# Drawn rows of V fetched by SyncE transfers with a register for the row, keys in natural order, steps in a new order

## The chip, the cores and the metric

One NeuronCore of a Trainium2 chip. The metric is the device time of one execution in microseconds (us): the median of three executions.

## The reference, cut to what matters

Block-sparse attention over 4 batches and 8 heads, and a feed-forward layer on its output. A block is 32 tokens, so a sequence of 768 has 24 blocks.

```python
scores = (1.0 / np.sqrt(D)) * np.matmul(q, k.transpose(0, 1, 3, 2))    # B, H, S, D = 4, 8, 768, 64
mask = np.abs(blk_i - blk_j) <= 1
mask = mask | (blk_i == 0) | (blk_j == 0) | (blk_i == n_blocks - 1) | (blk_j == n_blocks - 1)
for qb in range(n_blocks):
    for kb in sampled_blocks[qb]:                                      # three drawn blocks to a block
        mask[qb * block:(qb + 1) * block, kb * block:(kb + 1) * block] = True
...
attn_out = np.matmul(softmax(scores where mask), v)
x = attn_out.transpose(0, 2, 1, 3).reshape(B * S, H * D)               # 3072 x 512
h = x @ w_in                                                           # 512 x 2048
out = (h * np.cos(h)) @ w_out                                          # 2048 x 512
```

Which blocks are drawn is an input (`sampled_blocks`, 24 x 3), so their addresses are known only when the kernel runs.

## The kernel before

**Tiles.** The list `seq` has 24 tiles: in each of the 4 batches five sparse tiles of 128 query rows (four blocks, called groups below), and a dense one for the first and the last query block and what is left. Two tiles make a pair, and each pair goes through the feed-forward layer: up projection `ph` (line 1648), h*cos(h), down projection `po` (line 1745). Wide numbers are kept as two fp16 halves, a high and a low one, so most matmuls run on each half.

**A sparse tile.** The queries `U` meet 256 keys in each group: the two end blocks, a window of three blocks of its own, and three drawn blocks. `sparse_scores` (line 1367) writes the scores `sp` to PSUM, VectorE adds the mask `bias` (line 1394), ScalarE takes the exponential into `P` (line 1416), ScalarE and VectorE split it into the halves of `ring` (lines 1433 and 1437), a transposing transfer on SyncE brings `ring` to `PT` (line 1456), and TensorE multiplies PT by `V` (line 1467). The result is normalised and transposed to `xT` by another transfer on SyncE (line 1511), and `xT` feeds `ph`. The keys `W` come by transposing transfers (line 1183), once a batch.

**V.** Each batch's V is stored in DRAM as fp16 halves, in a scratch `scr[b]` with rows of 2 KB. A tile's 128 partitions of V are read from there, with the keys of a group in an order of even tokens and then odd ones:

- `v_ends` (lines 1308 to 1311): the two end blocks, in four SyncE transfers of 16 rows for four groups. A V buffer keeps them through its batch, so they are fetched only for the first two tiles of a batch: 32 transfers.
- `v_window` (lines 1313 to 1316): two SyncE transfers of 48 rows for four groups, 40 in all.
- `v_dense` (lines 1303 to 1306): two SyncE transfers for each dense tile, 8 in all.
- `v_gather` (lines 1318 to 1326): the drawn blocks, four GpSimd gathers of 96 rows to a sparse tile, 80 in all. Their row numbers come from the tile `gidx`, which VectorE makes at the start (`const_a`, line 1018 among it, and `const_gidx`).

There are two V buffers, and tile n takes buffer n % 2: a load for tile n must wait until tile n-2 has been multiplied by V. The keys of drawn blocks are copied on VectorE and ScalarE (line 1189), with their column taken from a register: the registers are loaded by TENSOR_LOAD (line 998), and an address step (FUSED_REGOPS) stands ahead of each copy.

**What sets the order.** A planner (`plan_kernel`, with the inner `gather_v` and `load_regs`) makes 3229 steps. The table `POS` gives each step, by its number, a place in one order over all engines; buffers are handed out in that order, and every engine's instructions are written in it. Each engine then works through its own in order, and an instruction whose data isn't there holds up all behind it on its engine. SyncE issues all transfers but the gathers.

Of the kernel before, what the change touches and what calls it, by code (L numbers as in the profile page):

```python
# [13 lines left out]
F32 = mybir.dt.float32  # L14
I32 = mybir.dt.int32
# [5 lines left out]
P = 128  # L21
# [14 lines left out]
XE = [4, 4, 4, 4, 4]  # L36
LPE = [0, 0, 0, 0, 0, 0, 0, 0, 0, 0, 0, 0, 0, 0, 0, 0]
# [1794 lines left out]
```

## Time and profile before

| | |
|---|---|
| three executions | 869.81, 871.02 and 859.93 us |
| the profiled execution | 861.11 us, of which the span (first to last instruction) is 859.2 us |
| granted TensorE clock, mean over the span | 0.910 of full speed |

An engine's busy share is over the span. The chain that ended last is followed back from the last instruction, at each step to what released it; its shares tell where the end was set. "issue" there is time in which an engine waited for nothing that the profile shows, SPq is SyncE's queue of instructions, and "DMA PT<-ring" is time in which the next piece of the chain waited for that transfer. All times of rows are from the one profiled execution. A row's share of the DMA queues is of the time of 16 DMA engines together.

### The profile page before, as it was taken

The page shows a single profiled execution, that of the slowest core. Times are in us where ns is not written, and L with a number is a line of the kernel's source. Part 1 is how long each engine was busy: PE and PEld are TensorE (multiplying, and loading weights), DVE is VectorE, ACT ScalarE, POOL GpSimd, SP SyncE. Part 2 cuts the span into 40 slices and gives each one's busy share as a digit, 9 for nine tenths or more (in the row PEclk, how much of TensorE's full clock was granted, in tenths as well). Part 3 has the DMA queues.
Part 4 walks back from the last instruction along what each step waited for, and adds up shares of the span by engine and source line. Part 5 has one row for each costly group of instructions (what it writes and reads, how often), then busy time and mean ns, then how long its engine had stood idle before and what let it go on. Part 6 is the DMA issues. An engine that isn't in the chain of part 4 may idle for free.

```text
span 859.2 us, 26549 instructions
## 1 busy us (share of the span) xinstructions
PE 711.9 (83%) x10953; PEld 488.2 (57%) x10953; DVE 549.6 (64%) x1619; ACT 597.5 (70%) x1214; POOL 97.8 (11%) x123
## 2 busy tenths in 40 slices
PE   3543579899878789898798988999987969999995
PEld 2433456575565447666465656667654647667662
DVE  4987989798748656785386756667735544644221
ACT  2686768789748778899397788688954746865220
POOL 4330122000200111000201110100110210000000
PEclk9755569899999899999899999999988989999998
DMA  7999998989999999999999999997979896742100
GB/s 270 276 278 227 185 223 180 210 170 201 239 178 168 193 176 219 210 192 168 189 169 196 178 209 185 204 168 128 197 112 161 114 159 111 140 99 50 37 13 29
DMA packets 239794, 146.34 MB, mean 170 GB/s; under 512 B 203952, under 2 KB 204080, under 8 KB 239664
## 3 DMA queue, kind: packets, MB, share of 16 engines
q1 hardware_dynamic: 234544, 128.83, 78.3%
q0 software_dynamic: 5120, 15.73, 8.3%
q8 instruction: 87, 1.43, 0.8%
q14 instruction: 43, 0.35, 0.2%
HBM read 77.67 MB, written 12.58 MB: 105 GB/s over the span
## 4 chain that ended last, share of the span: by engine, by line
PE 41%; DMA 20%; DVE 16%; ACT 10%; issue 8%; SPq 3%; another core or an unknown queue 1%; DVEq 0%; ACTq 0%
PE ph L1648 17%; PE po L1745 16%; DMA PT<-ring 7%; PE sp L1367 4%; ACT P L1416 3%; DMA U<-U 2%; DMA W<-kn 2%; DVE P L1394 2%; DVE ring L1437 2%; DMA xT<-n 2%; PE xp L1467 2%; DMA qs<-in_q_dram 2%; DVE w L1100 1%; ACT L1416 1%; DVE n L1100 1%
## 5 line engine op out<-in xcount | busy, mean ns | idle before, releaser
L1648 PE MATMUL ph<-xT,w 128*128 128x256 f16 x2304 | 281.5, 281 | 20.7 <-DMA xT<-n 7.4
L1745 PE MATMUL po<-w,g 128*128 128x512 f16 x1152 | 271.0, 386 | 0.8 <-issue 0.6
L1648 PEld LDWEIGHTS <-w 128*128 128x128 f16 x2304 | 229.9, 101 | 65.5 <-issue 21.4
L1745 PEld LDWEIGHTS <-g 128*128 128x128 f16 x1152 | 111.1, 99 | 125.9 <-issue 11.2
L1416 ACT ACTIVATE P<-P,sm 128x256 f32<-128x256 f32 (+1 forms) x224 | 139.3, 623 | 28.1 <-DVE sm L1411 16.2
L1321 POOL DMA_INDIRECT V<-scr,gidx x80 | 80.4, 1006 | 593.8 <-PE xp L1467 380.5
L1665 ACT ACTIVATE g<-ph,sm 128x512 f32<-128x512 f32 x96 | 72.8, 773 | 78.2 <-PE ph L1648 75.1
L1437 DVE TENSOR_TENSOR ring<-P,ring 128x512 f16<-128x512 f32 (+1 forms) x144 | 89.4, 628 | 58.9 <-ACT ring L1433 56.3
L1367 PE MATMUL sp<-W,U 128*32 128x192 f16 (+1 forms) x2560 | 68.7, 245 | 53.2 <-issue 29.2
L1671 DVE SCALAR_TENSOR_TENSOR hs<-ph,sm,g 128x512 f32<-128x512 f32 x80 | 59.1, 748 | 69.6 <-ACT g L1665 69.4
L1433 ACT CAST ring<-P 128x512 f16<-128x512 f32 (+1 forms) x144 | 80.2, 567 | 22.4 <-DMA PT<-ring 20.2
L1367 PEld LDWEIGHTS <-U 128*32 128x32 f16 x2560 | 50.0, 107 | 71.6 <-issue 68.1
L1394 DVE CUSTOM_DVE_ANT_1 P<-sp,bias 128x256 f32<-128x256 f32 x160 | 61.5, 419 | 44.4 <-PE sp L1367 30.0
L1736 DVE TENSOR_TENSOR g<-hs,g 128x1024 f16<-128x1024 f32 x48 | 58.6, 1220 | 18.8 <-ACT g L1733 18.5
L1733 ACT ACTIVATE g<-hs 128x1024 f16<-128x1024 f32 x48 | 50.3, 1050 | 21.4 <-DVE hs L1671 21.3
L1467 PE MATMUL xp<-V,PT 128*32 128x64 f16 x3840 | 45.3, 201 | 22.1 <-DMA PT<-ring 14.1
L1467 PEld LDWEIGHTS <-PT 128*32 128x32 f16 x3840 | 38.7, 98 | 34.3 <-DMA PT<-ring 15.4
L1416 ACT ACTIVATION_READ_ACCUMULATOR P<-P,sm 128x1 f32 x224 | 41.8, 187 | 0.0
L1394 DVE CUSTOM_DVE_ANT_1 P<-sp,dbias 128x384 f32<-128x384 f32 x64 | 35.1, 552 | 6.7 <-PE sp L1378 4.4
L1665 ACT ACT_TABLE_LOAD x29 | 37.2, 1283 | 0.5
L1097 ACT ACTIVATE kn<-stage,sm 128x256 f16<-128x256 f32 (+1 forms) x41 | 20.3, 526 | 23.1 <-DMA W<-kn 12.4
L1416 ACT ACT_TABLE_LOAD x28 | 35.9, 1283 | 0.5
(165 smaller groups left out, 683.1 us busy)
## 6 DMA issues: line engine op xcount, KB each, us to landing
V<-scr SPq DMA_DIRECT2D x40, 384.0 KB
stage<-in_k_dram SPq DMA_DIRECT2D x12, 512.0 KB
w<-in_moe_w_in_dram SPq DMA_DIRECT2D x12, 512.0 KB
w<-in_moe_w_out_dram SPq DMA_DIRECT2D x12, 512.0 KB
V<-scr SPq DMA_DIRECT2D x8, 768.0 KB
scr<-n SPq DMA_DIRECT2D x21, 256.0 KB
qs<-in_q_dram SPq DMA_DIRECT2D x20, 256.0 KB
U<-U SPq DMA_DIRECT2D x40, 128.0 KB
```

The lines of the kernel that those rows point to most:

```text
L1321: self.nc.gpsimd.indirect_dma_start(self.v_groups(V)[:96, j, 0, :], None, self.scr[b][:, :], bass.IndirectOffsetOnAxis(ap=self.gidx[:, c : ...
L1367: mm(o, U[:, z, h, rows], k, start=(a == 0 and z == 0 and part == 0), stop=(a == 1 and z == 1 and part == 1), tile_position=(0, BLK * j),)
L1394: self.nc.vector.tensor_tensor_reduce(out=self.head_cols(n, a, Pt).rearrange("p (n c) -> p n c", c=hf), in0=self.head_cols(n, a, sp).rearr ...
L1416: self.nc.scalar.activation(Pv, Pv, AF.Exp, scale=qc[:, 4:5], bias=nb[:, bcol : bcol + 1], accum_out=sums[:, 2 * j + a : 2 * j + a + 1],)
L1433: self.nc.scalar.copy(hi, p)
L1437: self.nc.vector.tensor_tensor(lo, p, hi, ALU.subtract)
L1467: mm(xp[32 * j : 32 * j + 32, h, :], PT[:, 4 * a + 2 * l + c, 32 * j : 32 * j + 32], V[:, j, c, h, d0:d1], start=(a == 0 and c == 0 and x ...
L1648: self.nc.tensor.matmul(ph[:, ff, :], self.W1[p][:, wl, cc, c * P : (c + 1) * P], xT[:, xl * NCC + cc, :], start=(j == 0), stop=(j == len( ...
L1665: self.nc.scalar.activation(self.half_cols(g, h), ph.rearrange("p f t -> p (f t)"), AF.Sin, scale=self.turns[b][:, p : p + 1], bias=self.h ...
L1671: self.nc.vector.scalar_tensor_tensor(self.half_cols(hs, h), ph.rearrange("p f t -> p (f t)"), c, self.half_cols(g, h), op0=ALU.mult, op1= ...
L1736: self.nc.vector.tensor_tensor(g[:, 1024:2048], hs, g[:, 0:1024], ALU.subtract)
L1745: self.nc.tensor.matmul(po, g[:, gl, ff, t * P : (t + 1) * P], self.W2[p][:, wl, ff, :], start=(first and ff == half * hf and j == 0), sto ...
```

## The change

- **Drawn rows.** In place of a gather of 96 rows, three SyncE transfers of 32 rows (64 KB) each, one to a drawn block: `v_drawn`, 12 to a sparse tile, 240 in all. Each takes its source row from a register, and in front of each SyncE has one address step ("ISA" in the order).
- **Registers.** SyncE loads them by TENSOR_LOAD: for each of the five sparse tiles of a batch nine that are kept for the whole kernel (`SPR = 9`), and three that are loaded anew for each of the 20 sparse tiles. 25 loads. `const_regs` makes the rows of the drawn blocks (`sv`) with one more instruction; `const_gidx` and ten instructions of `const_a` go.
- **Natural order of keys.** An end block comes by one transfer of 32 rows (two to a tile, 16 in all), and a window's transfer has consecutive rows. So that scores meet V in this order, `sparse_scores` writes the even and the odd keys of drawn blocks and windows to every second column of PSUM, and `bias` is laid out to suit.
- **Order.** `POS` is a new table, of 3397 steps, and the orders of all engines differ from those before.

```diff
+SPR = 9
 POS = [
...
 def gather_v(n, pos):
         if i < 2:
             for x in range(2):
-                for y in range(2):
-                    op("SP", 0, pos, lambda x=x, y=y: e.v_ends(n, V.t, x, y), r=[scr[b]], w=[(V, ("e", x, y))], dma=0.3, name=f"vg{n}_1")
+                op("SP", 0, pos, lambda x=x: e.v_ends(n, V.t, x), r=[scr[b]], w=[(V, ("e", x))], dma=0.8, name=f"vg{n}_1")
...
         for j in range(4):
-            op("POOL", 1.03, ipos + 0.8 + j * 0.5, lambda j=j: e.v_gather(n, V.t, j), r=[scr[b], gidx], w=[(V, ("d", j))], dma=1.5, name=f"vi{n}_{j}")
+            for s in range(3):
+                x = 3 * j + s
+                if x == SPR:
+                    load_regs(i, 4, [by["ksc0s"], *[o for o in pl.ops[-400:] if o.name.startswith(f"vi{n - 1 - (n % 6 == 0)}_3_")]], ipos + 0.8)
+                op("SP", 0, ipos + 0.8 + j * 0.5, lambda j=j, s=s: e.v_drawn(n, V.t, j, s), r=[scr[b], regs[i, 3 + (x >= SPR)]], w=[(V, ("d", j, s))], dma=0.35, hw=0.5, name=f"vi{n}_{j}_{s}")
...
+    for i in range(NS):
+        load_regs(i, 3)
     load_v(0, pr["V0"])
...
+        nc.vector.tensor_scalar(self.sv, self.sx, BLK, None, op0=ALU.mult)
...
 def v_rows(self, b, tok, n, j=0):
-        return bass.AP(src.tensor, src.offset, [[2 * self.HD, n], [j * self.HD, 4], [1, self.HD]])
+        return bass.AP(src.tensor, src.offset, [[self.HD, n], [j * self.HD, 4], [1, self.HD]])
...
-    def v_ends(self, n, V, e, y):
-        b, hf = self.seq[n][0], BLK // 2
-        p = (96, 0)[e] + hf * y
-        self.nc.sync.dma_start(self.v_groups(V)[p : p + hf, :, e], self.v_rows(b, (self.S - BLK) * e + y, hf))
+    def v_ends(self, n, V, e):
+        b, p = self.seq[n][0], (96, 0)[e]
+        self.nc.sync.dma_start(self.v_groups(V)[p : p + BLK, :, e], self.v_rows(b, (self.S - BLK) * e, BLK))
...
-    def v_gather(self, n, V, j):
+    def v_drawn(self, n, V, j, s):
         b, i = self.seq[n]
-        c = 4 * i + j
-        self.nc.gpsimd.indirect_dma_start(
-            self.v_groups(V)[:96, j, 0, :],
-            None,
-            self.scr[b][:, :],
-            bass.IndirectOffsetOnAxis(ap=self.gidx[:, c : c + 1], axis=0),
-        )
+        to = self.v_groups(V)[BLK * s : BLK * s + BLK, j, 0, :]
+        x = 3 * j + s
+        reg = self.regs[i, 3][x] if x < SPR else self.regs[i, 4][x - SPR]
+        self.nc.sync.dma_start(to, self.scr[b][bass.ds(reg, BLK), :])
...
 def sparse_scores(self, n, unit, U, sp):
-                            o = bass.AP(t.tensor, t.offset, [list(t.ap[0]), [48, 2], [160, 2], [1, 48]])
+                            o = bass.AP(t.tensor, t.offset, [list(t.ap[0]), [1, 2], [160, 2], [2, 48]])
```

What the order makes of it is shown at three places of SyncE's queue. The first is its start. `stage` and `hs` take inputs (keys and v), `w1` the weights, `sm` the registers' source. Before:

```order
1 L1237 DMA qs0_93<-in_q_dram 128x512
2 L961 DMA xT0_111<-in_sampled_blocks_dram 128x144
3 L1142 DMA stage0_78<-in_k_dram 128x1024
4 L1142 DMA stage1_79<-in_k_dram 128x1024
5 L1546 DMA w1_3_67<-in_moe_w_in_dram 128x1024
6 L1142 DMA stage2_80<-in_k_dram 128x1024
7 L1546 DMA w1_3_67<-in_moe_w_in_dram 128x1024
8 L1142 DMA hs0_82<-in_v_dram 128x1024
```

and after:

```order
1 L1225 DMA qs0_92<-in_q_dram 128x512
2 L972 DMA xT0_110<-in_sampled_blocks_dram 128x144
3 L1130 DMA stage0_77<-in_k_dram 128x1024
4 L1130 DMA stage1_78<-in_k_dram 128x1024
5 L1130 DMA stage2_79<-in_k_dram 128x1024
6 L1530 DMA w1_3_67<-in_moe_w_in_dram 128x1024
7 L1010 TENSOR_LOAD sm_76
8 L1130 DMA hs0_81<-in_v_dram 128x1024
```

A load of registers stands seventh, ahead of the load of v into hs0, and all three loads of keys stand ahead of the weights.

The second place is the change from batch 0 to batch 1, where the first key transposes (W<-kn) of the new batch are issued. Loads of V for tiles 6 and 7 go to V0 and V1. Before:

```order
134 L1142 DMA stage0_78<-in_v_dram 128x1024
135 L1311 DMA V1_110<-scr1_126 16x4x1024 x2
136 L1237 DMA qs0_93<-in_q_dram 128x512
137 L1511 DMA_TRANSPOSE xT1_112<-n160_90 128x8x128
138 L1183 DMA_TRANSPOSE W_63<-kn0_88 128x4x128 x2
139 L1183 DMA_TRANSPOSE W_63<-kn1_89 128x4x128 x2
140 L1316 DMA V0_109<-scr1_126 48x4x1024
```

and after:

```order
262 L1310 ISA
263 L1310 DMA V0_108<-scr1_125 32x1024
264 L1310 ISA
265 L1310 DMA V0_108<-scr1_125 32x1024
266 L1753 DMA out_0_dram<-kn0_87 128x512
267 L1225 DMA qs0_92<-in_q_dram 128x512
268 L1310 ISA
269 L1310 DMA V1_109<-scr1_125 32x1024
270 L1310 ISA
271 L1310 DMA V1_109<-scr1_125 32x1024
272 L1303 DMA V0_108<-scr1_125 48x4x1024
273 L1171 DMA_TRANSPOSE W_63<-kn1_88 128x4x128 x2
```

Before, end rows of V, queries and an xT transpose came ahead of the first key transposes, and the drawn rows were on GpSimd. Now four drawn pieces (32x1024) and a window (48x4x1024) stand there.

The third is inside a batch, at tile 8's transposes of the probabilities (PT<-ring). Before:

```order
181 L1456 DMA_TRANSPOSE PT1_106<-ring1_102 128x8x128
182 L1456 DMA_TRANSPOSE PT3_108<-ring3_104 128x8x128
183 L1511 DMA_TRANSPOSE xT0_111<-n161_91 128x8x128
184 L1316 DMA V1_110<-scr1_126 48x4x1024
185 L1277 DMA U0_94<-U0_94 64x1024
186 L1316 DMA V1_110<-scr1_126 48x4x1024
187 L1237 DMA qs0_93<-in_q_dram 128x512
188 L1226 DMA scr2_127<-n160_90 128x1024
```

and after:

```order
372 L1440 DMA_TRANSPOSE PT1_105<-ring1_101 128x8x128
373 L1010 TENSOR_LOAD sm_76
374 L1310 ISA
375 L1310 DMA V1_109<-scr1_125 32x1024
376 L1265 DMA U1_94<-U1_94 64x1024
377 L1495 DMA_TRANSPOSE xT0_110<-n160_89 128x8x128
378 L1310 ISA
379 L1310 DMA V1_109<-scr1_125 32x1024
380 L1263 DMA U1_94<-U1_94 64x1024
381 L1440 DMA_TRANSPOSE PT0_104<-ring0_100 128x8x128
```

Between two PT transposes there are now a load of registers and two drawn pieces of V, with an address step in front of each; the xT transpose stands behind one of them.

## Rows read from the trace of the kernel before

**Rows 1.** Page, part 1, busy time of each engine.

```profile
PE 711.9 (83%) x10953; PEld 488.2 (57%) x10953; DVE 549.6 (64%) x1619; ACT 597.5 (70%) x1214; POOL 97.8 (11%) x123
```

**Rows 2.** Page, part 4, the chain that ended last, by engine and by line.

```profile
PE 41%; DMA 20%; DVE 16%; ACT 10%; issue 8%; SPq 3%; another core or an unknown queue 1%; DVEq 0%; ACTq 0%
PE ph L1648 17%; PE po L1745 16%; DMA PT<-ring 7%; PE sp L1367 4%; ACT P L1416 3%; DMA U<-U 2%; DMA W<-kn 2%; DVE P L1394 2%; DVE ring L1437 2%; DMA xT<-n 2%; PE xp L1467 2%; DMA qs<-in_q_dram 2%; DVE w L1100 1%; ACT L1416 1%; DVE n L1100 1%
```

**Rows 3.** Waits of the engines for V: us in total, times, longest.

```profile
PE xp L1467 <- DMA V<-scr: 4.9, 2, 4.4
PEld L1467 <- DMA V<-scr: 4.5, 1, 4.5
```

**Rows 4.** Timeline of SyncE, first and last of its 478 transfers: start, us.

```profile
0.72 0.42 SPq L1237 DMA_DIRECT2D qs<-in_q_dram  x1
...
807.36 41.33 SPq L1769 DMA_DIRECT2D out_dram<-ot  x5
```

**Rows 5.** Tile V, loads: duration ns min/median/max, first and last start us.

```profile
L1316 SPq DMA_DIRECT2D V<-scr x40: 313/572/1444, 48.8 to 702.5; - x40
L1311 SPq DMA_DIRECT2D V<-scr x32: 303/532/1628, 46.9 to 649.5; - x32
L1306 SPq DMA_DIRECT2D V<-scr x8: 427/462/526, 177.6 to 731.8; - x8
```

**Rows 6.** Tile PT, its transposes on SyncE.

```profile
L1456 SPq DMA_TRANSPOSE PT<-ring x140: 960/1280/6934, 59.9 to 784.4; - x140
```

**Rows 7.** Page, part 5, groups: count | busy us, mean ns | idle before.

```profile
L1321 POOL DMA_INDIRECT V<-scr,gidx x80 | 80.4, 1006 | 593.8 <-PE xp L1467 380.5
...
L1367 PE MATMUL sp<-W,U 128*32 128x192 f16 (+1 forms) x2560 | 68.7, 245 | 53.2 <-issue 29.2
```

**Rows 8.** Lines 998 and 1189, register loads and address steps.

```profile
L998 DVEq TENSOR_LOAD <-sm x10: 961/968/2150, 7.2 to 299.5; - x10
L998 ACTq TENSOR_LOAD <-sm x5: 1753/1764/1948, 7.1 to 25.9; - x5
...
L1189 DVEq FUSED_REGOPS  x164: 57/57/65, 42.0 to 669.9; - x164
```

**Rows 9.** Waits of SyncE's own queue.

```profile
SPq L1456 <- DVE ring L1437: 53.3, 22, 8.1
...
SPq L1316 <- PE xp L1467: 8.0, 3, 3.8
```

**Rows 10.** The chain in order of time: start us, us, engine, line.

```profile
114.94 7.89 DMA xT<-n
...
236.79 10.96 DMA W<-kn
250.34 5.05 DMA W<-kn
...
318.49 3.10 DMA xT<-n
...
555.55 5.06 DMA xT<-n
...
680.84 11.18 DMA PT<-ring
...
740.22 5.06 DMA PT<-ring
```

**Rows 11.** Page, part 3, DMA queues: packets, MB, share of 16 engines.

```profile
q1 hardware_dynamic: 234544, 128.83, 78.3%
q0 software_dynamic: 5120, 15.73, 8.3%
```

**Rows 12.** Timeline of GpSimd: start, us, line, tiles [idle before <-releaser].

```profile
228.77 0.92 POOL L1321 DMA_INDIRECT V<-scr,gidx  x1 [78.69 <-PE sp L1128]
...
237.78 0.92 POOL L1321 DMA_INDIRECT V<-scr,gidx  x1 [0.30 <-issue]
```

**Rows 13.** Line 1018, one of VectorE's small instructions at the start.

```profile
L1018 DVE TENSOR_SCALAR xT<-xT x1: 153/153/153, 11.3 to 11.3; 128x1 f32<-128x1 f32 x1
```

More of the change, by code (lines that the diff above doesn't have):

```diff
@@ L369, in plan_kernel @@
     Vs = [Val(None, t) for t in e.vbufs]
-    bias, dbias, gidx = (Val() for _ in range(3))
+    bias, dbias = (Val() for _ in range(2))
     regs = {}
@@ L374, in plan_kernel, with load_regs @@
     op("DVE", 0.15, -400, lambda: e.const_regs(tmp.t), r=[(tmp, 0)], w=[sxv], name="sx")
-    def load_regs(i, which, after=()):
+    def load_regs(i, which, after=(), pos=0.0):
         regs[i, which] = Val()
         x = pr["XD"][i]
-        eng, cost, p = (("DVE", 0.05 + 0.236 * XE[i], pr["RG"][i]), ("ACT", 0.05 + 0.236 * (12 - XE[i]), pr["RA"][i]), ("DVE", 0.05 + 0.236 * (x - XE[i]), 200.0 + i))[which]
+        eng, cost, p = (("DVE", 0.05 + 0.236 * XE[i], pr["RG"][i]), ("ACT", 0.05 + 0.236 * (12 - XE[i]), pr["RA"][i]), ("DVE", 0.05 + 0.236 * (x - XE[i]), 200.0 + i), ("SP", 0.05 + 0.236 * SPR, -200.0 + i), ("SP", 0.05 + 0.236 * (12 - SPR), pos))[which]
         op(eng, cost, p, lambda: e.load_regs(i, which), r=[sxv], w=[regs[i, which]], name=f"regs{i}_{which}", after=after)
@@ L386, in plan_kernel @@
     op("DVE", 0.7, -298, lambda: e.const_a(tmp.t), r=[(tmp, "pid")], w=[(tmp, "a")], name="const_a")
-    op("DVE", 0.3, pr["CG"], lambda: e.const_gidx(tmp.t), r=[(tmp, "a"), (tmp, 0)], w=[gidx], name="const_gidx")
     op("DVE", 0.8, pr["CG"], lambda: e.const_samples(tmp.t), r=[(tmp, 0)], w=[(tmp, "smp")], name="const_samples")
@@ L858 @@
     KD, KX = 192, 576
-    SMALL = 296 + 72 + 24
+    SMALL = 296 + 144 + 24
     kv = wc = None
@@ L899, in __init__ @@
         self.junk = pool.tile([P, 512], BF16, name="junk")
-        self.gidx = pool.tile([96, 4 * self.NS], I32, name="gidx")
         self.bias = pool.tile([P, self.NS, 16], BF16, name="bias")
@@ L943, in __init__ @@
         self.bcol = {x: self.col(1) for x in "abcd"}
-        self.sx = self.col(3 * self.NB).bitcast(I32)[0:1]
+        self.sx, self.sv = (self.col(3 * self.NB).bitcast(I32)[0:1] for _ in range(2))
         self.k_src, self.wi, self.wo = k, w_in.bitcast(I32), w_out.bitcast(I32)
@@ L998, in load_regs @@
         self.regs[i, which] = self.nc.values_load_multi_w_load_instructions(
-            self.sx[0:1, x + (0, XE[i], XE[i])[which] : x + (XE[i], 12, d)[which]],
-            engines=[(ENG.DVE, ENG.Activation, ENG.DVE)[which]],
+            (self.sx, self.sv)[which > 2][0:1, x + (0, XE[i], XE[i], 0, SPR)[which] : x + (XE[i], 12, d, SPR, 12)[which]],
+            engines=[(ENG.DVE, ENG.Activation, ENG.DVE, ENG.SP, ENG.SP)[which]],
             min_val=0,
-            max_val=(self.S - BLK) // 2,
+            max_val=(self.S - BLK) // (1 if which > 2 else 2),
             skip_runtime_bounds_check_because="the indices were clamped to the blocks that there are",
@@ L1007, in const_a @@
         nc, NB = self.nc, self.NB
-        pid, low, third, jint = (self.tv(t, 320 + x, 1) for x in range(4))
-        self.lowf, thirdf, jf = (self.tv(t, 324 + x, 1, dt=F32) for x in range(3))
+        pid, jint, jf = self.tv(t, 320, 1), self.tv(t, 323, 1), self.tv(t, 326, 1, dt=F32)
         self.jf = jf
-        nc.vector.tensor_scalar(low, pid, 15, None, op0=ALU.bitwise_and)
-        nc.vector.tensor_scalar(third, pid, 4, None, op0=ALU.arith_shift_right)
         nc.vector.tensor_scalar(jint, pid, 5, None, op0=ALU.arith_shift_right)
-        nc.vector.tensor_copy(self.lowf, low)
-        nc.vector.tensor_copy(thirdf, third)
         nc.vector.tensor_copy(jf, jint)
-        odd = self.tv(t, 327, 1, dt=F32)
-        nc.vector.tensor_scalar(odd, thirdf, 3.0, None, op0=ALU.is_ge)
-        nc.vector.scalar_tensor_tensor(thirdf, odd, -3.0, thirdf, op0=ALU.mult, op1=ALU.add)
-        nc.vector.scalar_tensor_tensor(self.lowf, self.lowf, 2.0, odd, op0=ALU.mult, op1=ALU.add)
-        self.sel = [self.tv(t, 536 + x, 1, dt=F32) for x in range(3)]
-        for x in range(3):
-            nc.vector.tensor_scalar(self.sel[x], thirdf, float(x), float(BLK), op0=ALU.is_equal, op1=ALU.mult)
         self.cf = self.tv(t, 352, NB, dt=F32)
         nc.vector.tensor_copy(self.cf, self.tv(t, 328, NB))
-    def const_gidx(self, t):
-        n = 4 * self.NS
-        g, h = (self.tv(t, 544 + 24 * x, n, 96, dt=F32) for x in range(2))
-        own = [self.sampled(t, slice(0, 96))[:, 1 : 1 + n, x] for x in range(3)]
-        sel = [x[:96] for x in self.sel]
-        self.nc.vector.tensor_scalar(g, own[0], sel[0], self.lowf[:96], op0=ALU.mult, op1=ALU.add)
-        self.nc.vector.scalar_tensor_tensor(h, own[1], sel[1], g, op0=ALU.mult, op1=ALU.add)
-        self.nc.vector.scalar_tensor_tensor(self.gidx, own[2], sel[2], h, op0=ALU.mult, op1=ALU.add)
     def const_b1(self, t):
@@ L1038, in const_b1 @@
         nc.gpsimd.memset(bias[:, :, 6:16], 0.0)
-        nc.gpsimd.tensor_scalar(
-            bias[:, 0, 10:16].rearrange("p (z c) -> p z c", z=2)[:, :, 0:1],
-            jf.unsqueeze(1).to_broadcast([P, 2, 1]), 0.0, -BIG, op0=ALU.is_equal, op1=ALU.mult
-        )
+        nc.gpsimd.tensor_scalar(bias[:, 0, 10:12], jf.to_broadcast([P, 2]), 0.0, -BIG, op0=ALU.is_equal, op1=ALU.mult)
     def const_b(self, t):
@@ L1063, in const_b @@
             nc.gpsimd.tensor_scalar(
-                bias[:, :, 3 * z : 3 * z + 3], dup, 0.5, -BIG, op0=ALU.is_gt, op1=ALU.mult
+                bias[:, :, z:6:2], dup, 0.5, -BIG, op0=ALU.is_gt, op1=ALU.mult
             )
@@ L1315, in v_window @@
         p = 32 + 48 * y
-        self.nc.sync.dma_start(self.v_groups(V)[p : p + 48, :, 1], self.v_rows(b, 4 * BLK * i + y, 48, BLK))
-    def v_gather(self, n, V, j):
+        self.nc.sync.dma_start(self.v_groups(V)[p : p + 48, :, 1], self.v_rows(b, 4 * BLK * i + 48 * y, 48, BLK))
+    def v_drawn(self, n, V, j, s):
         b, i = self.seq[n]
-        c = 4 * i + j
-        self.nc.gpsimd.indirect_dma_start(
-            self.v_groups(V)[:96, j, 0, :],
-            None,
-            self.scr[b][:, :],
-            bass.IndirectOffsetOnAxis(ap=self.gidx[:, c : c + 1], axis=0),
-        )
+        to = self.v_groups(V)[BLK * s : BLK * s + BLK, j, 0, :]
+        x = 3 * j + s
+        reg = self.regs[i, 3][x] if x < SPR else self.regs[i, 4][x - SPR]
+        self.nc.sync.dma_start(to, self.scr[b][bass.ds(reg, BLK), :])
     def k_gather(self, n, Wg, h0, h1, which):
@@ L1362, in sparse_scores @@
                         if part == 0:
-                            o = bass.AP(t.tensor, t.offset, [list(t.ap[0]), [48, 2], [160, 2], [1, 48]])
+                            o = bass.AP(t.tensor, t.offset, [list(t.ap[0]), [1, 2], [160, 2], [2, 48]])
                             k = self.drawn_and_window(h, i, j)
                         else:
-                            o, k = t[:, 96:160].rearrange("p (n y c) -> p y n c", n=2, y=2), ends
+                            o, k = t[:, 96:160].rearrange("p (n c y) -> p y n c", n=2, y=2), ends
                         mm(
```

261 rows, old and new, of the table POS are left out of this document.

## The prediction

> **What bounds the kernel now.** I read the page's busy shares first: TensorE works 711.9 of the 859.2 us span [rows 1]. No engine fills the span, so I went on to the chain that ended last: TensorE has 41% of it, DMA 20%, SyncE's own queue 3% [rows 2]. By line the up and down projections lead it (PE ph and PE po), and the largest thing that isn't TensorE is the transpose of the probabilities, "DMA PT<-ring", with 7%. So time is lost where a transpose or a copy lands late, not where an engine is short of hours. What the change moves, the fetch of the drawn rows of V, shows in the waits twice. TensorE's matmuls and weight loads wait for V 4.9 and 4.5 us in all [rows 3]; GpSimd waits for a V buffer to come free (380.5 us on one reader, in the group of the gathers [rows 7]), which harms nobody. So the gathers are hardly late for their own reader. The questions are what they do to others, and what SyncE can still take.
>
> SyncE is the queue that the change loads. Its timeline has 478 transfers, of which the first and the last row stand in [rows 4]; their issue times add up to 519 us, nearly all of it before 735 us (the last load of V starts at 731.8 [rows 5]): 71% of that stretch. Tile 7's final transpose starts at 318.49 and tile 15's at 555.55 [rows 10], so a tile takes 237.1 / 8 = 29.6 us, and SyncE issues for 519 / 24 = 21.6 us of it. A PT transpose has a median of 1.28 us and a maximum of 6.9 [rows 6]: part of the 21.6 us is SyncE held up by transfers that are still in work.
>
> **The change part by part.** *GpSimd.* 80 gathers go, 80.4 us [rows 7]. Nobody waits for GpSimd's hours, so this alone gives nothing.
>
> *SyncE.* Added are 240 transfers of 32 rows, 12 to a sparse tile. No row shows a transfer whose source row is in a register. The nearest are the other loads of V from the same scratch, ends and windows: medians 0.532 and 0.572, from 0.303 to 1.628 us [rows 5]. I take 0.55: 132 us (73 to 391). The address step in front of each takes VectorE 57 ns [rows 8]; at 0.05, 12 us. Registers are loaded 25 times; four cost 0.968 and eight 1.764 us on other engines [rows 8], so 0.2 each and 0.17 to begin with: nine cost 1.97, three 0.77, and 5 x 1.97 + 20 x 0.77 = 25 us. Away go 16 of the 32 end transfers, 8.5 us. Together +161 us: 680 of 735 us, 92% where it was 71%, and in a sparse tile 21.6 + 8.05 = 29.7 us of a 29.6 us period. How much of it falls on the path? None, if it lies in the 216 us that SyncE has free; all 161 at the other end. The chain has 3% of 859.2 = 26 us of SyncE's queue for 519 us of issue, 5%. A transfer meets a busy queue 0.92 / 0.71 = 1.3 times as often, so 680 x 5% x 1.3 = 44 us against 26: **+18 us**.
>
> *What waits in the queue.* A drawn transfer that waits now stands in SyncE's order, and behind it the PT and xT transposes for which TensorE waits. Mostly SyncE finds its data ready: PT waited on "DVE ring" in 22 of 140 cases, 53.3 us, and windows of V waited for their buffer in 3 cases, 8.0 us [rows 9]. The drawn transfers of a tile share one such wait, 20 tiles against 40 windows: **+4 us** (0, to 16 if each tile has 0.8 more).
>
> *The DMA engines.* The gathers' queue q0 moves 15.73 MB in 8.3% of 16 engines, 71 us; at q1's mean (128.83 MB in 78.3%) the same bytes take 82 us [rows 11]. The bytes stay, so I take 0, between -11 and +11. What changes is when they run. A tile's four gathers start as soon as the buffer is free, whatever SyncE has in work; eight of two tiles run from 228.77 to 238.70 [rows 12], beside a key transpose that lands after 10.96 us [rows 10]. On the chain I took the 19 pieces between 100 and 800 us that are transposes, copies of U or loads of q. Nine have a gather issued during them or in the 3 us ahead; they last 7.81 us in the mean (first 114.94, last 680.84). Ten have none: 5.62 us (first 250.34, last 740.22) [rows 10]. Excess: 9 x 2.19 = 20 us. After the change the same bytes stand between the transposes, in pieces, where the order puts them; part of the delay stays, since at the batch's change four drawn pieces and a window stand in front of the first key transposes. I take half: **-10 us** (0 to -20).
>
> A page of the Trainium skill speaks against this gain. "DMA: Bandwidth & Descriptors", section "Issuing engines are not separate DMA queues", has all transfers run on the same 16 DMA engines, whoever issues them, so that a second issuing engine only saves the sequencer's time. By it the relief is nothing and SyncE's hours remain: a rival, below. That the trace agrees can't be said yet: 7.81 and 5.62 us are means over different transfers.
>
> *TensorE.* Scores of drawn and window keys are now written to every second column. No row shows such a write; scores are 4% of the chain [rows 2], 34 us, so 0, or +34 if each took twice as long. I take 0, the value of the nearest row: the 2560 score matmuls of the two widths keep count and size [rows 7].
>
> *The start.* Twelve small instructions of VectorE go, of the size of 153 ns [rows 13]: -2 to 0, I take **-1**. The first register load makes SyncE wait for VectorE until some 7 us [rows 8] and then takes 1.97 us, with a load of v and one of weights behind it; the key loads ahead of it keep the DMA engines at work meanwhile. Without that cover it would cost some 4 us.
>
> *The sum.* 18 + 4 + 0 - 10 + 0 - 1 = +11 us. The profiled execution took 861.1 us, so **872 us**. That is 1.3% over it, and 0.3% over the median of the runs shown, 869.8, two of which lie at 870 and one at 860.
>
> **The rivals.**
>
> *SyncE is full (slower).* 29.7 us of work in a 29.6 us tile leaves no room for waits, and what SyncE waits for, VectorE's second half of the probabilities above all, doesn't come earlier. SyncE now has 216 us free in 735. If between a third and a half of it stays as waits, SyncE needs 680 + 72 to 680 + 108 = 752 to 788 us where 735 were, +17 to +53; I take +35, **896 us**. It decides from the point where SyncE's issue and waits pass the tile's 29.6 us. For it: the sum is there before any wait is counted. Against it: part of the 519 us is SyncE held up by transfers in work, and the small pieces give those time to finish.
>
> *The gathers were the price (faster).* All of the 20 us comes back, the 9 us that TensorE waits for V go too, the start gives 2, and half of SyncE's 18 hides in its free time: 861 - 20 - 9 - 2 + 9 = **839 us**. For it: six of the nine longest of the 19 pieces have gathers beside them. Against it: of the seven PT pieces among them only three met one.
>
> *No relief (same).* The long pieces are long from the load of all transfers together, which stays; then 861 + 18 + 4 - 1 = **882 us**. This is what the page's rule gives. For it: q0 and q1 together hold 87% of the 16 engines' span, whoever issues.
>
> *Score writes cost twice (slower).* 861 + 34 = **895 us**. No row speaks for it and none excludes it.
>
> **How the numbers follow.** About 2% is what a measurement of this kernel can tell from no change. The forecast, 855 to 885 us by its own bounds (SyncE's +18 halved or grown by half, the relief between 0 and -20), has 0.32; no relief 0.10; SyncE full 0.32; score writes 0.04; the gathers as the price 0.22. So faster 0.22, same 0.42, slower 0.36. The range for 8 in 10 takes in 839 below and most of the way to 861 + 53 = 914 above: 838 to 910.
>
> **What would show it.** Right: SyncE's issue times add up to 650 to 690 us; the median of the V rows stays near 0.55 us; DMA's share of the chain falls below 20% and SyncE's queue rises above 3%; pieces of the nine's kind shorten towards 5.6 us. A full queue would show as PT transposes issued long after VectorE wrote "ring", as a share of "DMA PT<-ring" in the chain above the 7% of [rows 2], and as tiles wider than 29.6 us. Dear score writes would show in the score matmuls' nanoseconds alone. The forecast is wrong if the tiles' pace moves by more than 0.6 us, or if the first transpose of a tile's output on the chain, at 114.94 us [rows 10], moves by more than 10 us, for which no term speaks.

## The result, and the profile after

The changed kernel takes 816.84 us in the median of four executions, the kernel before 867.07 us beside it: a ratio of 0.944, with an interval of 0.936 to 0.951. The forecast was 872 us, with a range that began at 838. The kernel before varies by 2% between sets of runs (medians of 852 to 867 us), the changed one hardly (817 us again in a second set); every ratio below is within its own set.

The page of the changed kernel, parts 1, 3 and 4:

```profile
PE 713.5 (88%) x10953; PEld 500.7 (62%) x10953; DVE 549.3 (67%) x1607; ACT 602.5 (74%) x1218; POOL 15.9 (2%) x43
...
q1 hardware_dynamic: 245808, 144.57, 87.7%
...
PE 58%; DVE 15%; DMA 11%; ACT 6%; issue 5%; SPq 3%; DVEq 1%; ACTq 0%
PE po L1729 23%; PE ph L1632 22%; DMA PT<-ring 7%; PE sp L1351 6%; PE xp L1451 3%; DVE P L1378 2%; ACT P L1400 2%; DVE ring L1421 1%; PE sp L1362 1%; PE xp L1466 1%; DMA V<-scr 1%; SPq L1440 1%; DVE w L1088 1%; DVE n L1088 1%; DMA qs<-in_q_dram 1%
```

TensorE is as busy as before [rows 1], but its idle time fell from 859.2 - 711.9 = 147 us to 814.0 - 713.5 = 100.5. On the chain DMA went from 20% to 11%, TensorE from 41% to 58%, and SyncE's queue stayed at 3% [rows 2]. Such a chain is that of one execution: a second profile of the changed kernel, of the same time, has "DMA PT<-ring" at 3% in place of 7%. The bytes of the gathers moved from q0 to q1: 128.83 + 15.73 MB before [rows 11], 144.57 now.

The transfers of V in the changed kernel, by their tile (line 1310 the drawn pieces, 1303 the windows, 1298 the ends; MOVE is one of the two instructions of the address step, the other stands below):

```profile
L1310 SPq MOVE V<-scr x240: 29/29/38, 46.9 to 709.6; - x120
L1310 SPq DMA_DIRECT2D V<-scr x240: 315/326/1865, 47.0 to 709.7; - x120
L1303 SPq DMA_DIRECT2D V<-scr x40: 323/422/1812, 49.8 to 710.0; - x40
L1298 SPq DMA_DIRECT2D V<-scr x16: 410/550/1872, 49.3 to 620.1; - x16
```

The rest of the address steps and the register loads by their lines, PT's transposes by their tile, and SyncE's longest wait ahead of them:

```profile
L1310 SPq FUSED_REGOPS  x240: 37/37/51, 46.6 to 709.5; - x120
```

```profile
L1010 SPq TENSOR_LOAD <-sm x25: 669/927/2089, 6.9 to 701.8; - x25
```

```profile
L1440 SPq DMA_TRANSPOSE PT<-ring x140: 1209/1257/5449, 63.9 to 749.1; - x140
```

```profile
SPq L1440 <- DVE ring L1421: 27.9, 13, 7.4
```

A drawn piece holds SyncE for 0.326 us in the median, not the 0.55 that I took. The pieces add up to 101.7 us over the timeline, the two instructions of the address steps to 9.0 + 7.1 = 16, the register loads to 28: the five of nine registers took 1.87 to 2.09 us each, twelve of the twenty of three registers 0.67 to 0.71, the others up to 1.73. All SyncE transfers that aren't V took 472 us before and take 417 now; the PT transposes, whose median hardly moved [rows 6], went from 245 to 207 us, so it is their long ones that went. SyncE's total is 559 + 28 + 16 = 603 us, where 680 was forecast.

The final transposes of tiles 1, 7 and 15 in SyncE's timeline after:

```profile
115.10 1.30 SPq L1495 DMA_TRANSPOSE xT<-n  x1
...
301.52 1.29 SPq L1495 DMA_TRANSPOSE xT<-n  x1
...
527.18 1.26 SPq L1495 DMA_TRANSPOSE xT<-n  x1
```

The first stands where it stood (114.94 [rows 10]); from tile 7 to 15 a tile takes (527.2 - 301.5) / 8 = 28.2 us where it took 29.6, a move of 1.4 where the prediction named 0.6 as a sign of being wrong. The gain grows over the run, though not at every tile: 17 us by tile 7, 28 by tile 15, 18 by tile 16, 38 by the last.

The windows of the profile show what that does to TensorE (us; then busy time and instructions of PE, PEld, DVE, ACT, POOL; granted clock, DMA share, GB/s). Before:

```profile
100.00:200.00 100.00, 84.42 (x1441) 62.09 (x1442) 86.19 (x212) 79.05 (x154) 12.90 (x11) 0.85 0.94 193
...
400.00:500.00 100.00, 87.34 (x1455) 58.10 (x1454) 60.09 (x218) 70.56 (x167) 12.89 (x14) 0.93 1.04 185
...
600.00:700.00 100.00, 86.15 (x1571) 56.24 (x1564) 54.06 (x185) 67.19 (x143) 12.25 (x13) 0.93 0.90 147
```

and after:

```profile
100.00:200.00 100.00, 82.68 (x1480) 61.83 (x1481) 91.44 (x231) 87.80 (x176) 0.00 (x0) 0.95 1.06 212
...
400.00:500.00 100.00, 97.16 (x1675) 66.64 (x1673) 64.78 (x224) 90.87 (x189) 0.00 (x0) 1.00 1.02 190
...
600.00:700.00 100.00, 100.00 (x1710) 70.13 (x1699) 56.75 (x164) 70.09 (x133) 0.00 (x0) 1.00 0.84 165
```

In the two later stretches TensorE idles less, and its granted clock is 1.00, the level of 2.4 GHz, throughout, where it was 0.93 in the mean. The same projections also take less time each: ph 274 ns in place of 281, po 381 in place of 386, in the mean of the run, 16 us of TensorE in all. Its busy time is the same as before only because the score matmuls, below, got longer.

### The profile page after: what moved, and what is told of

It reads as the page before. It is cut to its first block, busy times and chain, and to the rows that moved or that the text cites. A ratio compares the mean times of both kernels' runs of the same rounds, so it can differ in the third digit from the quotient of the medians.

```text
span 814.0 us, 27168 instructions
## 1 busy us (share of the span) xinstructions
PE 713.5 (88%) x10953; PEld 500.7 (62%) x10953; DVE 549.3 (67%) x1607; ACT 602.5 (74%) x1218; POOL 15.9 (2%) x43
## 3 DMA queue, kind: packets, MB, share of 16 engines
q1 hardware_dynamic: 245808, 144.57, 87.7%
## 4 chain that ended last, share of the span: by engine, by line
PE 58%; DVE 15%; DMA 11%; ACT 6%; issue 5%; SPq 3%; DVEq 1%; ACTq 0%
PE po L1729 23%; PE ph L1632 22%; DMA PT<-ring 7%; PE sp L1351 6%; PE xp L1451 3%; DVE P L1378 2%; ACT P L1400 2%; DVE ring L1421 1%; PE sp L1362 1%; PE xp L1466 1%; DMA V<-scr 1%; SPq L1440 1%; DVE w L1088 1%; DVE n L1088 1%; DMA qs<-in_q_dram 1%
## 5 line engine op out<-in xcount | busy, mean ns | idle before, releaser
L1632 PE MATMUL ph<-xT,w 128*128 128x256 f16 x2304 | 270.3, 274 | 4.4 <-DMA xT<-n 3.2
L1729 PE MATMUL po<-w,g 128*128 128x512 f16 x1152 | 266.3, 381 | 3.9 <-issue 3.9
L1632 PEld LDWEIGHTS <-w 128*128 128x128 f16 x2304 | 223.7, 98 | 46.8 <-issue 7.8
L1351 PE MATMUL sp<-W,U 128*32 128x64 f16 (+1 forms) x2560 | 93.2, 331 | 16.6 <-DVE sm L1378 12.4
L1351 PEld LDWEIGHTS <-U 128*32 128x32 f16 x2560 | 71.1, 135 | 34.5 <-issue 27.2
L1451 PE MATMUL xp<-V,PT 128*32 128x64 f16 x3840 | 42.7, 200 | 9.8 <-DMA PT<-ring 6.2
L1177 ACT COPY W<-W 128x256 f16 (+1 forms) x112 | 33.8, 377 | 3.5 <-PE sp L1351 1.8
L1362 PE MATMUL sp<-W,U 128*128 128x384 f16 x128 | 30.6, 326 | 5.4 <-DVE sm L1378 3.9
```

Source lines behind the costliest of these rows:

```text
L1351: mm(o, U[:, z, h, rows], k, start=(a == 0 and z == 0 and part == 0), stop=(a == 1 and z == 1 and part == 1), tile_position=(0, BLK * j),)
L1451: mm(xp[32 * j : 32 * j + 32, h, :], PT[:, 4 * a + 2 * l + c, 32 * j : 32 * j + 32], V[:, j, c, h, d0:d1], start=(a == 0 and c == 0 and x ...
L1632: self.nc.tensor.matmul(ph[:, ff, :], self.W1[p][:, wl, cc, c * P : (c + 1) * P], xT[:, xl * NCC + cc, :], start=(j == 0), stop=(j == len( ...
L1729: self.nc.tensor.matmul(po, g[:, gl, ff, t * P : (t + 1) * P], self.W2[p][:, wl, ff, :], start=(first and ff == half * hf and j == 0), sto ...
```

## The experiments

**Order and transfers apart.** The change is two things: other transfers, and another order of all steps. `POS` was made anew for these kernels from rules, which the diffs show in place of its numbers; in them `old` and `new` are a step's place in the table of the kernel before and of the changed one. First the transfers in the old order, a piece where its gather stood:

```diff
-place["vi{n}_{j}_{s}"] = new
+place["vi{n}_{j}_{s}"] = old["vi{n}_{j}"] + 0.01 * s
```

> The changed kernel's code, but the order of steps of the kernel before: every step that both kernels have stands where it stood there, each three drawn pieces stand where their gather stood, register loads just ahead of the first pieces that need them. Theory A, the gathers were the price (they made all other transfers late, and the new order only fits the new pieces): most of the gain is there, 815 to 840 us, mean landing of the probabilities' transposes (PT) near 4.4 us. Theory B, the new order made the gain: 860 to 890 us, and DMA stays near 20% of the chain. Both halves needed: between 840 and 860.

Measured: 1.038 (1.032 to 1.045), 883 us, within the 860 to 890 of theory B. Its waits show why it is slower than the kernel before (us in total, times, longest):

```profile
PEld L1451 <- DMA V<-scr: 64.2, 20, 11.7
PE xp L1451 <- DMA V<-scr: 63.3, 21, 11.6
```

TensorE now waits for V once a tile, where it waited 4.9 us in all [rows 3]. A gather's place in the order meant little: GpSimd had little else to do and mostly waited for the buffer to come free [rows 7]. A piece on SyncE starts when its turn comes.

The reverse, gathers in the new order, once with natural keys and once with nothing but the order changed:

```diff
-op("SP", 0, ipos + 0.8 + j * 0.5, lambda j=j, s=s: e.v_drawn(n, V.t, j, s), r=[scr[b], regs[i, 3 + (x >= SPR)]], w=[(V, ("d", j, s))], dma=0.35, hw=0.5, name=f"vi{n}_{j}_{s}")
+op("POOL", 1.03, ipos + 0.8 + j * 0.5, lambda j=j: e.v_gather(n, V.t, j), r=[scr[b], gidx], w=[(V, ("d", j))], dma=1.5, name=f"vi{n}_{j}")
...
-place["vi{n}_{j}_{s}"] = new
+place["vi{n}_{j}"] = min(new["vi{n}_{j}_{s}"] for s in range(3))
```

> The changed kernel's order, natural order of keys and score writes, but the drawn rows again by 80 GpSimd gathers of 96 rows, each where the first of its three pieces stood; no registers on SyncE. Theory A (gathers were the price): it goes back to 850 to 870 us, the mean landing of the PT transposes back above 5 us and SyncE's PT transposes back to some 245 us in all. Theory B (the order): 805 to 825 us, SyncE has 100 us less to issue and nothing else changes.

> The kernel before with nothing changed but the order of its steps: every step stands where the changed kernel has it, a gather where the first of its three pieces stands. Theory B (the order made most of the gain): ratio 0.96 to 0.98 to the kernel before. Theory A (gathers were the price, and the order fits the new pieces alone): 0.99 to 1.02. If the cost of the score writes was hidden by the time that TensorE waited for, it is no faster than the run with gathers and natural keys in the new order, 0.97.

Measured: 0.974 (0.965 to 0.982) and 0.983 (0.976 to 0.989), 830 and 842 us: the first between the two theories, the second just outside theory B's range. So the order alone, gathers kept, gives some 2%, which is clear of no change, and the rest of the 4.5 to 5.6% needs the transfers. SyncE's PT transposes came to 229 and 236 us, against 207: part of that goes with the gathers.

Natural keys alone, in the kernel before with its gathers and its order (two of the edited places; the ends, windows and mask follow):

```diff
-return bass.AP(src.tensor, src.offset, [[2 * self.HD, n], [j * self.HD, 4], [1, self.HD]])
+return bass.AP(src.tensor, src.offset, [[self.HD, n], [j * self.HD, 4], [1, self.HD]])
...
-o = bass.AP(t.tensor, t.offset, [list(t.ap[0]), [48, 2], [160, 2], [1, 48]])
+o = bass.AP(t.tensor, t.offset, [list(t.ap[0]), [1, 2], [160, 2], [2, 48]])
```

> The kernel before in its own order with gathers, but with keys in natural order: 16 transfers for the ends in place of 32, and scores written to every second column. The score matmuls go to about 385 and 285 ns, 25 us more busy on TensorE. If they are hidden where TensorE waited anyway (137 us of idle time): ratio 0.99 to 1.01. If they fall on the path: 1.02 to 1.03.

Measured: 0.999 (0.991 to 1.007). The score writes cost nothing here, as below. The chain of this kernel, with the time, the order and the gathers of the kernel before:

```profile
PE 53%; DMA 16%; DVE 14%; ACT 7%; issue 6%; SPq 2%; another core or an unknown queue 1%; DVEq 0%; ACTq 0%
```

So TensorE's share can rise from 41% to 53%, and DMA's fall from 20% to 16%, without any gain in time.

Then the transfers in the old order at fairer places, all behind the windows, or spread, and the changed kernel once more, with no edit:

```diff
-place["vi{n}_{j}_{s}"] = new
+place["vi{n}_{j}_{s}"] = sorted(old["vg{n}_0"])[j // 2] + 0.01 * (3 * j + s)
...
-place["vi{n}_{j}_{s}"] = new
+place["vi{n}_{j}_{s}"] = sp_steps[int((3 * j + s) * len(sp_steps) / 12)] + 0.1
```

All other steps stand at their old places in the first two; `sp_steps` are the places of SyncE's other transfers there.

> The changed kernel's code in the order of the kernel before, as in the run with the pieces at the gathers' places, but with a tile's twelve drawn pieces right behind its two window transfers, six to each. There TensorE waited 63 us for V. If these waits were the loss: they fall below 15 us and the ratio goes from 1.04 to 0.96 to 0.99. If SyncE's queue itself is the loss (550 us of issue in an order made for 519): the ratio stays at 1.02 or above with other waits in their place, PT or xT.

> The old order with drawn transfers again, but a tile's twelve pieces spread evenly among SyncE's transfers from its first window on through seven tenths of the way to the first use of V. Theory C: from the 1.011 of the pieces behind the windows down to 0.98 to 0.995. Rival: 1.00 to 1.02, as before.

> The changed kernel itself, beside the kernels it is to be compared with. Both theories: about 0.944 to 0.96 of the kernel before, since the runs of the kernel before differ by 2% between sets.

Measured: 1.011 (1.006 to 1.016), 1.004 (1.000 to 1.008) and 0.955 (0.950 to 0.960). The expectations of 0.96 to 0.99 for the first and 0.98 to 0.995 for the second were both missed, and the first is under the 1.02 of its rival too: TensorE's matmuls' waits for V fell from 63 us to 10 and 17, but others came. The chain with the pieces behind the windows:

```profile
PE 44%; DMA 23%; DVE 13%; SPq 8%; ACT 6%; issue 4%; DVEq 0%; ACTq 0%
PE ph L1632 17%; PE po L1729 16%; DMA PT<-ring 10%; PE sp L1351 6%; DMA V<-scr 4%; SPq L1310 3%; PE xp L1451 2%; DMA scr<-n 2%; DVE ring L1421 2%; DVE P L1378 2%; SPq L1440 1%; DMA w<-in_moe_w_out_dram 1%; DVE n L1088 1%; PE xp L1466 1%; PE sp L1362 1%
```

SyncE's queue is 8% of it, 3% by the pieces' own line 1310, where it is 3% in the changed kernel; PT has 10%. This is like the rival "SyncE is full", in the old order and at a smaller price: yet here too the transfers that aren't V took only 420 us of SyncE. All runs show this, summed over their timelines: 405 to 434 us with pieces and 451 to 474 with gathers, whichever the order. So that SyncE is held up less isn't the gain by itself.

| drawn rows | old order | new order |
|---|---|---|
| gathers, old keys | 1 | 0.983 (0.976 to 0.989) |
| gathers, natural keys | 0.999 (0.991 to 1.007) | 0.974 (0.965 to 0.982) |
| transfers | 1.004 to 1.038, by their places | 0.944 (0.936 to 0.951), 0.955 (0.950 to 0.960) |

**Pieces together.** In the new order the 240 pieces stand in 126 groups among the other transfers, 63 of them of a single piece and the longest of six. Four runs put a tile's pieces together, as twelve at the place of the seventh or of the first, as two clumps of six, as four of three (k is a piece's rank among the twelve):

```diff
-place["vi{n}_{j}_{s}"] = new
+place["vi{n}_{j}_{s}"] = sorted(new["vi{n}"])[6] + 0.01 * (3 * j + s)
...
-place["vi{n}_{j}_{s}"] = new
+place["vi{n}_{j}_{s}"] = sorted(new["vi{n}"])[0] + 0.01 * k
...
-place["vi{n}_{j}_{s}"] = new
+place["vi{n}_{j}_{s}"] = sorted(new["vi{n}"])[6 * (k // 6) + 3] + 0.01 * (k % 6)
...
-place["vi{n}_{j}_{s}"] = new
+place["vi{n}_{j}_{s}"] = sorted(new["vi{n}"])[3 * (k // 3) + 1] + 0.01 * (k % 3)
```

> The changed kernel with one thing moved: the twelve drawn pieces of a tile stand one behind the other, where the seventh of them stood, in place of singly among the other transfers. Theory C (transfers pay only where the order spreads them, a clump of twelve holds SyncE for 5 us and the PT and xT transposes behind it wait): ratio 0.97 to 0.99, and PT or V waits of TensorE up by 10 us or more. Rival (the place of the pieces doesn't matter much, what pays is the rest of the new order): 0.95 to 0.965.

> The changed kernel with the twelve pieces of a tile together at the place of the first of them, as early as the order allows. If a clump of twelve costs wherever it stands: 1.00 to 1.03, as where the seventh stood. If only that one place collided with transposes: 0.96 to 0.98.

> The changed kernel with the twelve pieces of a tile in two clumps of six, each at the place of its fourth piece. Three together cost nothing, twelve cost 6%. If the cost grows with the time that SyncE is held beyond what the transposes behind it can stand (six pieces, 2.5 us): between, 0.965 to 0.985. If it sets in only near twelve: 0.945 to 0.96. If it sets in above three: 0.99 to 1.01.

> The changed kernel with the twelve pieces of a tile in four clumps of three: each three that follow one another in the order stand together at the place of the middle one. If a clump costs by the time that it holds SyncE (three pieces 1.3 us, twelve 5 us): about a quarter of what twelve cost, ratio 0.965 to 0.975. If any move away from the places that the order gives costs as much: 0.99 or above. If short clumps are free: 0.95 to 0.96.

Measured: twelve 1.014 (1.006 to 1.022) and, at the other place, 1.003 (0.998 to 1.007); six 0.967 (0.960 to 0.975); three 0.947 (0.942 to 0.951), as good as the changed kernel. A clump of twelve takes back all, at either place, more than I had put on it at the seventh's; the price grows with the clump's length. SyncE's timeline at tile 8 shows a part of how. With twelve together, where the seventh stood:

```profile
309.85 1.69 SPq L1440 DMA_TRANSPOSE PT<-ring  x1
311.75 7.08 SPq L1310 DMA_DIRECT2D V<-scr  x12
319.00 2.64 SPq L1440 DMA_TRANSPOSE PT<-ring  x2
```

and the same transposes in the changed kernel:

```profile
304.28 1.34 SPq L1440 DMA_TRANSPOSE PT<-ring  x1
305.83 1.03 SPq L1310 DMA_DIRECT2D V<-scr  x2
306.97 2.62 SPq L1440 DMA_TRANSPOSE PT<-ring  x2
309.78 1.93 SPq L1310 DMA_DIRECT2D V<-scr  x4
```

With twelve together the two PT transposes behind the pieces start 9.2 us after the one ahead of them, in the changed kernel 2.7 us. What waits meanwhile is `ring`, which ScalarE can't fill again before its transpose has been made. The changed kernel, then twelve at the seventh's place, then twelve at the first's:

```profile
ACT ring L1417 <- DMA PT<-ring: 17.9, 15, 3.3
```

```profile
ACT ring L1417 <- DMA PT<-ring: 51.8, 21, 7.2
```

```profile
ACT ring L1417 <- DMA PT<-ring: 22.2, 13, 5.1
```

So the ring's waits go with the clump at the seventh's place and not with that at the first's, which loses nearly as much with hardly more of them than the changed kernel. There SyncE's own queue stands on the chain, half of it by the pieces' line, where it has 3% in the changed kernel:

```profile
PE 58%; DMA 11%; SPq 10%; DVE 10%; issue 5%; ACT 4%; DVEq 0%; ACTq 0%
PE ph L1632 22%; PE po L1729 22%; SPq L1310 5%; PE sp L1351 5%; PE xp L1451 3%; DMA PT<-ring 3%; PE sp L1362 2%; DVE P L1378 2%; DMA U<-U 2%; DMA V<-scr 1%; DMA W<-kn 1%; PE xp L1466 1%; SPq L1440 1%; SPq L1010 1%; DMA w<-in_moe_w_in_dram 1%
```

At the seventh's place the pieces also wait more for earlier loads of V than in the changed kernel (at the first's they don't: 0.9 us). SyncE's waits, changed kernel and twelve:

```profile
SPq L1310 <- DMA V<-scr: 3.8, 3, 2.3
```

```profile
SPq L1310 <- DMA V<-scr: 11.8, 6, 2.7
```

At tile 8 the twelve held SyncE for 7.1 us without such a wait. Two pieces that follow one another start 0.50 us apart there: 0.32 for the transfer, 0.07 for the address step, and the rest between the instructions. The load of three registers among them took 0.68 us.

**Which part of the order.** Up to the end of tile 3 the one order, from there on the other (transfers; the old order with pieces behind the windows):

```diff
-place = new
+place = old if old < old_end_of_tile_3 else 1e6 + new
...
-place = new
+place = new if new < new_end_of_tile_3 else 1e6 + old
```

> Drawn transfers; up to the end of tile 3 (some 165 us) the old order with the pieces behind the windows, from there on the new order. If the old order loses at the start alone (there the pieces of two tiles meet the loads of k, v and weights; tile 2 was 10 us late): 1.00 to 0.99 at the most, as only the 10 us differ from 0.955: 0.965 to 0.975. If it loses all along: about half, 0.955 to 0.965.

> The counterpart: the new order up to the end of tile 3, from there on the old order with the pieces behind the windows. If the old order's loss with transfers is the start: 0.995 to 1.00 (10 to 14 us under the 1.011), and the new order's own gain, which the runs show to grow from tile to tile, is missing. If the start gives most of the gain: 0.96 to 0.98.

Measured: 0.982 (0.975 to 0.989) and 1.005 (1.002 to 1.009). The second is a little above what the first theory gave (0.995 to 1.00): it is ahead of the kernel before by 3 us at tile 3 and 13 at tile 7, and level with it from tile 13 on. The first lost more than expected: at tile 3 it is 8 us behind the changed kernel, at tile 4 already 19 to 21, and 22 at the last, so nearly all of its loss comes at the start and the seam, and the split is not clean.

**The score writes.** The old columns, contiguous runs of 48, with the changed kernel else as it is. The scores then no longer stand in the order of the mask and of V, so this run is for the time alone:

```diff
-o = bass.AP(t.tensor, t.offset, [list(t.ap[0]), [1, 2], [160, 2], [2, 48]])
+o = bass.AP(t.tensor, t.offset, [list(t.ap[0]), [48, 2], [160, 2], [1, 48]])
...
-o, k = t[:, 96:160].rearrange("p (n c y) -> p y n c", n=2, y=2), ends
+o, k = t[:, 96:160].rearrange("p (n y c) -> p y n c", n=2, y=2), ends
```

> The changed kernel with the scores written to PSUM in the columns of the kernel before (runs of 48 next to each other instead of every second column), so the columns no longer stand in the order of the keys of V and of the mask. If writing to every second column is what lengthens the score matmuls: the 192-wide ones go from 381 to about 277 ns and the 64-wide from 281 to about 212, TensorE's busy time falls by some 20 us, and as TensorE is 58% of the chain the time falls by 10 to 20 us, to 797 to 807. If the lengthening has another cause (the clock, the order): nanoseconds and time stay, 812 to 821.

and the natural columns written one after the other, the keys read alternately:

```diff
-o = bass.AP(t.tensor, t.offset, [list(t.ap[0]), [1, 2], [160, 2], [2, 48]])
+o = bass.AP(t.tensor, t.offset, [list(t.ap[0]), [160, 2], [2, 48], [1, 2]])
...
-[self.KX, 2], [self.KD + 64 * i + hf * j - 48 * j, 2], [1, 48]])
+[self.KD + 64 * i + hf * j - 48 * j, 2], [1, 48], [self.KX, 2]])
...
```

> The changed kernel with the two inner loops of each sparse score matmul exchanged: the columns are written one after the other, and the even and odd keys, which lie apart in W, are read alternately. Same result in the same places. If the cost sits in the writes: as with the old columns, near 277 and 212 ns, and 797 to 807 us. If it comes with any stride, read or written: the matmuls stay near 381 and 281 ns or get longer, and 812 us or more.

The score matmuls by form, 192 and 64 keys wide (busy us, mean ns), in the kernel before, the changed one, with the old columns, and with alternate reading:

```profile
L1367 PE MATMUL sp<-W,U 128*32 128x192 f16 x1280 | 64.5, 277 | 41.5 <-issue 17.5 <-DVE sm L1394 10.3 <-DMA U<-U 7.3
L1367 PE MATMUL sp<-W,U 128*32 128x64 f16 x1280 | 56.3, 212 | 11.7 <-issue 11.7
```

```profile
L1351 PE MATMUL sp<-W,U 128*32 128x192 f16 x1280 | 89.9, 381 | 16.6 <-DVE sm L1378 12.4 <-DVE W L1177 1.5 <-ACT W L1177 1.3
L1351 PE MATMUL sp<-W,U 128*32 128x64 f16 x1280 | 83.2, 281 | 0.0
```

```profile
L1351 PE MATMUL sp<-W,U 128*32 128x192 f16 x1280 | 56.4, 273 | 29.0 <-DVE sm L1378 19.6 <-DMA U<-U 4.5 <-DVE W L1177 2.5
L1351 PE MATMUL sp<-W,U 128*32 128x64 f16 x1280 | 49.9, 210 | 0.7 <-issue 0.7
```

```profile
L1351 PE MATMUL sp<-W,U 128*32 128x192 f16 x1280 | 89.1, 346 | 20.1 <-DVE sm L1378 16.0 <-ACT W L1177 2.2 <-DVE W L1177 1.8
L1351 PE MATMUL sp<-W,U 128*32 128x64 f16 x1280 | 77.9, 224 | 0.0
```

Between the changed kernel and the old columns, which differ in nothing else, a write to every second column lengthens the wide matmul from 273 to 381 ns and the narrow one from 210 to 281, as between the kernel before and the changed one; reading alternately instead takes back part of it (346 and 224), which neither expectation held. The time doesn't care: 816.6 us with the old columns, where 797 to 807 was expected, and 819.5 with alternate reading, beside 817 for the changed kernel. With the old columns TensorE is 713.5 - 686.9 = 27 us less busy and idles 27 us more. So a share of 58% on the chain was no promise that time taken off TensorE comes back.

## Why the prediction was wrong

- **The step that failed: the sum over edits with the order left at nothing.** I priced transfers, registers, waits and writes, and counted the new order only where it put a piece in front of something. The order alone gives about 2%, 13 us, and it decides what the transfers are worth: 1.004 to 1.038 for them in the old order, +3 to +33 us where the sum had +11, and 0.944 to 0.955 in the new, 817 us where gathers in that order take 830. So the sum was fair for the old order, in which the change wasn't made. No term and no rival held that.
- **SyncE, +18 us: mis-sized twice.** Its issue grew by 603 - 519 = 84 us, not by 161. The pieces took 101.7 us in place of 132 (0.326 in the median, not 0.55), and the other transfers hold SyncE 55 us less, which I had mentioned only as an argument against the full queue; the register loads (28 us for 25) and the address steps (16 for 12) were about right. SyncE's queue is 3% of the chain, as before, and didn't rise; by that the term came to about nothing. The formula behind it, that a queue 1.3 times as full costs in proportion, doesn't hold: with about as much issue, the order moved the time from 817 to 866 us.
- **The waits, +4 us: wrong way.** PT's waits on "DVE ring" fell to 27.9 us in 13 cases from 53.3 in 22 [rows 9], in the new order; in the old one with the pieces behind the windows they are 47.3 in 19.
- **The relief, -10 us: the sign came, its worth isn't shown.** The chain's transfers of the kinds that I counted last 4.97 us in the mean (14 of them between 100 and 800 us), where the 19 of before lasted 6.66. But they are as short in the old order with the pieces behind the windows (4.43, 22 of them), where nothing was gained. DMA's fall on the chain, from 20% to 11%, is no measure either: the kernel with natural keys and gathers has 16% and no gain.
- **Score writes, 0: right for the time, by luck.** I took "the value of the nearest row"; the matmuls got a third longer, and TensorE's waiting hid it.
- **The start, -1 us: right, in part by luck.** The first transpose of a tile's output moved by 0.2 us, but the new order with gathers has it 6 to 11 us later (120.9 and 126.0, one profile each), and the prediction had no term for that.
- **On the page's rule.** The Trainium skill ("DMA: Bandwidth & Descriptors", "Issuing engines are not separate DMA queues") has all transfers run on the same 16 engines, whoever issues them, so that issuing from several engines saves only the sequencer's time. The rival "no relief", 882 us, is what I drew from it, and the runs don't bear that out: the bytes and the engines are the same, yet the other transfers were issued in 417 us in place of 451 in the new order. That it is the same 16 engines isn't contradicted; that the relief is nothing and SyncE's hours remain did not come out, with the packets' size and the starting times changed as well.
- **The rivals.** "SyncE is full" is what a poor order makes of the same transfers: 862 and 866 us with the pieces together, 883 at the gathers' places. "The gathers were the price" had the sign, with 839 us, and without the order it is wrong too: taking the gathers away in the old order gained nothing.

Why the gathers lengthen other transfers isn't settled: when they start, how their queue is served and the size of their packets all change together here. What in the new order gives its 2% with gathers kept isn't shown either. That it is the holding of SyncE that a clump costs, and not its bytes, rests on the timeline, the ring's waits for one clump and SyncE's share of the chain for the other, not on a run that separates the two.

## What to carry to other kernels

Work that moves from an engine with nothing else to do to a queue that is used in order isn't priced by its issue times: its place in the order decides, and twelve short transfers in a row cost 6% here where the same twelve in threes cost nothing. When a change comes with a new order, price the order as a part of its own, and try each part in the other's order before believing that either made the gain. And look at where the time would go before counting a saving on the busiest engine: 27 us less work on TensorE gave nothing here.

## What the runs showed of the hardware

- A transfer of 32 rows with its source row in a register holds SyncE for 0.326 us in the median, less than the windows of 48 rows in four groups (0.422), and the two instructions of its address step for 37 and 29 ns; in the clump at tile 8 such transfers start 0.50 us apart. A load of nine registers takes 1.87 to 2.09 us and one of three mostly 0.67 to 0.71: the line through two points of other engines gave 1.97 and 0.77.
- Scores written to every second PSUM column: 381 in place of 273 ns at 192 columns, 281 in place of 210 at 64.
- With gathers on GpSimd SyncE's other transfers take 451 to 474 us of its time, without them 405 to 434, at the same bytes, and whether or not the kernel is faster.
